# An attention backward kernel: transposing each key block's E in its own step, and X's transposes behind them

## The chip, the cores and the metric

The kernel runs on one core of one Trainium2 chip, as one launch. The metric is the device time of that launch in microseconds (us); less is better. The kernel before took 2694.29 us as the median of three runs (2686.12 to 2701.21).

## What is computed

The reference is a small block, forward and backward: a layer norm, 32-head attention `s`, a gated MLP `g`, and `x + s * g`, together with the gradients for `x`, the attention's weights and the MLP's weights. The part that matters here is the attention.

```python
B, S, D, H = 1, 2048, 512, 32          # Dh = 16
qkv = transpose((x @ wqkv).reshape(B, S, 3, H, Dh), 2, 0, 3, 1, 4)
scores = einsum("bhqd,bhkd->bhqk", q, k) * (Dh ** -0.5)
p = softmax(scores, axis=-1)
o = einsum("bhqk,bhkd->bhqd", p, v)
...
out, vjp = jax.vjp(f, A_x, A_wqkv, A_wo, B_w1, B_b1, B_w2, B_b2)
grads = vjp(grad_out)
```

The backward of attention needs, for every head, the products of two S x S matrices: the unnormalized softmax E, and G, which is E times the matrix of gradients d. Sums over keys (the output, the gradient of q) use them with keys on the partitions; sums over queries (the gradients of k and v) need them with queries on the partitions. So both matrices are made once and transposed once.

## The kernel before

The kernel has three stages: the projections and the MLP forward; the attention, forward and backward in one; the remaining gradients. Only the attention, `attention_core`, is touched. There the order of the instructions of each engine is the order in which the program issues them, written out by hand; the framework adds the waits for data and for buffers.

**Tiling.** Two heads make a pair; there are 16 pairs. 2048 queries are cut into 4 chunks `qc` of 512. A pair with a chunk is a block `j`, of which there are 64. In a block the 2048 keys are 16 key blocks `kb` of 128. One step `g` of the main loop deals with one key block (`j = g // 16`, `kb = g % 16`), so there are 1024 steps and a few more at the end to drain. Four key blocks make a key chunk `kc`.

**What one step issues**, for both heads `hj`, in this order:

- `emit_z(g + ZOFF)` (line 804): matmuls of an older block that add to `Z`, the gradients of k and v, from transposed G (`gk`, on even steps) and transposed E (`ek`, on odd steps). In 16 steps it goes through two halves `kp` of the keys with four query blocks `qb` each. `emit_acc` (lines 817 and 819, VectorE) adds a finished `Z` to `acc` every eighth step. After the last query chunk GpSimd copies the sum to `ob` and SyncE stores it.
- `emit_s(g + 1, 0)` (L629, L635): the scores of the next key block into a PSUM tile `s` of the pool `ps_st`, and ScalarE's exponential of it into the tile `et`, which holds E of one key chunk: 4 query blocks x 4 key blocks x 2 heads x 128.
- `emit_XT(g)`, once per block, at `g % 16 == FIN_AT`: four f32 transposes of `xs`, the sums over keys of the block that has just ended (L744), into a PSUM tile of the pool `ps_d`.
- `emit_d(g, 0)` and `emit_d(g, 1)` (L647): the matmul d of this key block, in tiles of `ps_d`; then `emit_s(g + 1, 1)`.
- `emit_mult(g)` (L660): VectorE writes G = d times E into `gts`, a tile for two key blocks.
- `emit_fin(g)`, once per block, at `FIN_AT`: VectorE copies XT into `xt` and makes reciprocals and factors (L756 to L770), GpSimd makes the weights `W1` and `W2` for Z and writes the block's output and gradient of q.
- `emit_T(g)` (L694): TensorE transposes of E, 128 x 128 each, into a tile of `ps_st`.
- `emit_x(g - 1, ...)` (L719, L722, L725): the sums over keys, into `X`; `emit_xs` (L734), once per block, copies X to `xs` on ScalarE.
- `emit_cT(g)` (L704): ScalarE copies the transposes from PSUM to `ek`.
- `emit_dmat(g)`: DMA transposes on SyncE's queue. After every second key block it transposes `gts` into `gk` (L674). After every fourth, it transposes one query block of `et` into an `ek` (L678), behind the `gk` of the same step.

**How E gets transposed before.** A key chunk has 4 query blocks x 8 squares (4 key blocks, 2 heads). Query block 3 goes by DMA. Query blocks 0 to 2 go over TensorE once the chunk is complete: `t_unit` shifts by four steps, so that step 4, 5 and 6 after the chunk's first step transpose query blocks 0, 1 and 2, eight squares each, and the fourth step transposes nothing.

**Buffers.** `ps_st` and `ps_d` have three PSUM tiles each, `ps_x` and `ps_z` one each. `et` comes from `etp` with 3 buffers, `gts` from `gtp` with 3, `gk` from `gbp` with 7, `ek` from `ekp` with 19, `xs` and `xt` have one each. `FIN_AT` is 2 and `ZOFF` is -21.

**Operands.** Those of the next pair are loaded during the second query chunk (`kb == 0 and qc == 1`): in five parts, four steps apart, three loads, GpSimd copies into `Pad`, a DMA transpose of it to `KVT`, copies again, and a DMA transpose to `QDT`.

Of the kernel before, what the change touches and what calls it, by code (L numbers as in the profile page):

```python
# [542 lines left out]
def attention_core(ctx, tc, NAT_s, NATQ_s, Oall, dQall, dKVT_out, ident_f32, ident_bf, npairs=16, nqc=4):  # L543
# [4 lines left out]
    ps_d = ctx.enter_context(tc.tile_pool(name="ps_d", bufs=3, space=PSUM))  # L548
    ps_x = ctx.enter_context(tc.tile_pool(name="ps_x", bufs=1, space=PSUM))
    ps_z = ctx.enter_context(tc.tile_pool(name="ps_z", bufs=1, space=PSUM))  # L550
    etp = sb("etp", 3)
    gtp = sb("gtp", 3)
    gbp = sb("gbp", 7)
    ekp = sb("ekp", 19)
    xsp = sb("xsp", 1)
    finp = sb("finp", 1)
    wp = sb("wp", 2)
# [51 lines left out]
    def a_unit(g):  # L609
        return (g // 16, g % 16) if 0 <= g < NSTEP else None  # L610
# [53 lines left out]
    def emit_dmat(g):  # L664
        a = a_unit(g)
        if a is None:
            return
        j, kb = a
        kc = kb // 4
        if kb % 2 == 1:  # L670
            h = (kb // 2) % 2
            if h == 0:
                blk[j]["Gk"][kc] = gbp.tile([128, 2, 16, 128], bf16, name="gk")
            nc.sync.dma_start_transpose(out=blk[j]["Gk"][kc][:, h], in_=st_gt[g][:].rearrange("k a h q -> k (a h q)"))  # L674
        if kb % 4 == 3:
            ek = ekp.tile([128, 8, 128], bf16, name="ek")
            blk[j]["Ek"][(kc, 3)] = ek
            nc.sync.dma_start_transpose(out=ek[:], in_=st_et[g][:, 3].rearrange("k a h q -> k (a h q)"))  # L678

    def t_unit(g):  # L680
        a = a_unit(g - 4)
        if a is None or a[1] % 4 == 3:
            return None
        return a[0], a[1] // 4, a[1] % 4

    def emit_T(g):
        u = t_unit(g)
        if u is None:
            return
        j, kc, qb = u  # L690
        et = st_et[j * 16 + kc * 4 + 3]
        t = ps_st.tile([128, 8, 128], bf16, name="tT", tag="st")
        for b in range(8):
            nc.tensor.transpose(t[:, b, :], et[:, qb, b // 2, b % 2, :], ident_bf[:])  # L694
        st_T[g] = t

    def emit_cT(g):
        u = t_unit(g)
        if u is None:
            return  # L700
        j, kc, qb = u
        ek = ekp.tile([128, 8, 128], bf16, name="ek")
        blk[j]["Ek"][(kc, qb)] = ek
        nc.scalar.copy(out=ek[:].rearrange("q a k -> q (a k)").bitcast(f32),  # L704
                       in_=st_T.pop(g)[:].rearrange("q a k -> q (a k)").bitcast(f32))

    def emit_x(g, part):
        a = a_unit(g)
# [19 lines left out]
    def emit_xs(g):  # L728
        a = a_unit(g)
        if a is None or a[1] != 15:  # L730
            return
        j = a[0]
        xs = xsp.tile([128, 512], f32, name="xs")
        nc.scalar.copy(out=xs[:], in_=blk[j].pop("X")[:])  # L734
        blk[j]["xs"] = xs

# [10 lines left out]
    def emit_fin(g):  # L747
        j = g // 16 - 1
        if g % 16 != FIN_AT or not 0 <= j < NB:
            return  # L750
        p, qc = blocks[j]
        NQq = op_of(j)["NATQq"]
        NQd = op_of(j)["NATQd"]
        XT = blk[j].pop("XT")
        xt = finp.tile([128, 4, 128], f32, name="xt")
        nc.vector.tensor_copy(out=xt[:], in_=XT[:])  # L756
        XTv = xt[:].rearrange("q b (r c) -> q b r c", r=4)
        W1 = wp.tile([128, 4, 2, 32], bf16, name="W1")
        W2 = wp.tile([128, 4, 2, 32], bf16, name="W2")
        nc.gpsimd.memset(W2[:, :, :, 0:16], 0.0)  # L760
        st0 = qc * 4
        nqs = NQq[:, st0:st0 + 4, :, 1:17]
        ndo = NQd[:, st0:st0 + 4, :, :]
        bc = lambda ap: ap.to_broadcast([128, 4, 2, 16])
        rL = finp.tile([128, 4, 2, 1], f32, name="rL")
        nc.vector.reciprocal(out=rL[:], in_=XTv[:, :, 2:4, 17:18])  # L766
        dl = finp.tile([128, 4, 2, 1], f32, name="dl")
        nc.vector.tensor_tensor(out=dl[:], in0=XTv[:, :, 2:4, 0:1], in1=rL[:], op=ALU.mult)
        ndr = finp.tile([128, 4, 2, 1], f32, name="ndr")
        nc.vector.scalar_tensor_tensor(out=ndr[:], in0=dl[:], scalar=-1.0, in1=rL[:], op0=ALU.mult, op1=ALU.mult)  # L770
        nc.gpsimd.tensor_tensor(out=W2[:, :, :, 16:32], in0=nqs, in1=bc(rL[:]), op=ALU.mult)  # L771
        nc.gpsimd.tensor_tensor(out=W1[:, :, :, 0:16], in0=ndo, in1=bc(rL[:]), op=ALU.mult)
        nc.gpsimd.tensor_tensor(out=W1[:, :, :, 16:32], in0=nqs, in1=bc(ndr[:]), op=ALU.mult)
        Ov = Oall[:, st0:st0 + 4, p * 32:(p + 1) * 32].rearrange("q b (h c) -> q b h c", h=2)
        nc.gpsimd.tensor_tensor(out=Ov, in0=XTv[:, :, 0:2, 16:32], in1=bc(rL[:]), op=ALU.mult)
        t1 = finp.tile([128, 4, 2, 16], f32, name="t1")
        nc.gpsimd.tensor_tensor(out=t1[:], in0=XTv[:, :, 0:2, 0:16], in1=bc(dl[:]), op=ALU.mult)
        nc.gpsimd.tensor_tensor(out=t1[:], in0=XTv[:, :, 2:4, 1:17], in1=t1[:], op=ALU.subtract)
        rL4 = finp.tile([128, 4, 2, 1], f32, name="rL4")
        nc.gpsimd.tensor_scalar(out=rL4[:], in0=rL[:], scalar1=0.25, scalar2=None, op0=ALU.mult)  # L780
        dQv = dQall[:, st0:st0 + 4, p * 32:(p + 1) * 32].rearrange("q b (h c) -> q b h c", h=2)
        nc.gpsimd.tensor_tensor(out=dQv, in0=t1[:], in1=bc(rL4[:]), op=ALU.mult)
        blk[j]["W1"] = W1
        blk[j]["W2"] = W2

    def emit_z(g):
        u = z_unit(g)
        if u is None:
            return
        j, kp, qb, part = u  # L790
        if part == 0 and qb == 0:
            blk[j]["Z"] = ps_z.tile([128, 512], f32, name="Z", tag="z")
        Z = blk[j]["Z"]
        for par in range(2):
            kc = 2 * kp + par
            if part == 0:
                W = blk[j]["W2"]
                mv = blk[j]["Gk"][kc][:].rearrange("q a (r h b) k -> q h b a r k", r=2, h=2)[:, :, qb]
            else:
                W = blk[j]["W1"]  # L800
                mv = blk[j]["Ek"].pop((kc, qb))[:].rearrange("q (a h) k -> q h a k", h=2)
            for hj in range(2):
                r = 64 * par + 32 * hj
                nc.tensor.matmul(Z[r:r + 32, :], lhsT=W[:, qb, hj, :], rhs=mv[:, hj],  # L804
                                 start=(part == 0 and qb == 0), stop=(part == 1 and qb == 3), skip_group_check=True,
                                 tile_position=(0, r))

    def emit_acc(g):
        u = z_unit(g)
        if u is None or u[2] != 3 or u[3] != 1:  # L810
            return
        j, kp = u[0], u[1]
        p, qc = blocks[j]
        Z = blk[j]["Z"]
        av = acc[:, kp, :]
        if qc == 0:
            nc.vector.tensor_copy(out=av, in_=Z[:])
        else:
            nc.vector.tensor_tensor(out=av, in0=Z[:], in1=av, op=ALU.add)  # L819
        if qc == nqc - 1:  # L820
            if kp == 0:
                cur["ob"] = outp.tile([128, 2, 512], bf16, name="ob")
            ob = cur["ob"]
            nc.gpsimd.tensor_copy(out=ob[:, kp, :], in_=av)
            if kp == 1:
                def store():
                    dv = dKVT_out[p * 64:(p + 1) * 64, :].rearrange("r (a b s) -> r a b s", a=2, b=2)
                    for b in range(2):
                        nc.sync.dma_start(out=dv[:, :, b, :], in_=ob[b * 64:(b + 1) * 64])
                late.append((cur["g"] + 2, store))  # L830

    FIN_AT = 2
    ZOFF = -21
    late = []
    for f in load_ops(0):
        f()
# [2 lines left out]
    for g in range(NSTEP + 16 + 8):  # L839
        cur["g"] = g  # L840
        a = a_unit(g)
        if a is not None:
            j, kb = a
            p, qc = blocks[j]
            if kb == 0 and qc == 1 and p + 1 < npairs:
                for i, f in enumerate(load_ops(p + 1)):
                    late.append((g + 1 + 4 * i, f))
        for it in [x for x in late if x[0] <= g]:
            late.remove(it)
            it[1]()  # L850
        emit_z(g + ZOFF)
        emit_acc(g + ZOFF)
        emit_s(g + 1, 0)
        emit_XT(g)
        emit_d(g, 0)
        emit_d(g, 1)
        emit_s(g + 1, 1)
        emit_mult(g)
        emit_fin(g)
        emit_T(g)  # L860
        emit_x(g - 1, "l")
        emit_x(g - 1, "e")
        emit_x(g - 1, "g")
        emit_xs(g - 1)
        emit_cT(g)
        emit_dmat(g)
        st_gt.pop(g - 2, None)
        st_et.pop(g - 12, None)
# [104 lines left out]
```

## Time and profile before

| | |
|---|---|
| median of three runs | 2694.29 us |
| the profiled execution | 2689.98 us |
| its span | 2688.2 us |
| mean granted TensorE clock | 0.957 |
| TensorE matmul, busy | 2294.1 us (85%) |
| VectorE, busy | 1898.4 us (71%) |
| ScalarE, busy | 1795.7 us (67%) |
| GpSimd, busy | 600.7 us (22%) |
| first and last d of the attention | 283.5 and 2072.9 us |

The profile shows one execution on the core. PE is TensorE's matmuls, PEld its loads of weights, DVE is VectorE, ACT ScalarE, POOL GpSimd, SP SyncE; SPq rows are DMAs that SyncE issues. "L694" is line 694 of the kernel. Rows of the groups read: line, engine, operation, what is written <- what is read, shapes, count | busy us, mean ns of one | idle time of the engine just ahead of them, and what ended it. Rows of the timeline read: start, duration, engine, line, operation, tiles, count and, in brackets, idle time with its releaser. A few of the attention's groups in the whole span:

```profile
L635 ACT ACTIVATE et<-s 128x512 bf16<-128x512 f32 x2048 | 1127.3, 596 | 247.9 <-PE s L629 136.7
L694 PE MATMUL tT<-ident_bf,et 128*128 128x128 bf16 x6144 | 475.2, 220 | 40.1 <-ACT ek L704 39.4
L704 ACT COPY ek<-tT 128x512 f32<-128x512 f32 x768 | 455.2, 593 | 0.5 <-PE tT L694 0.5
L725 PE MATMUL X<-gts,NAT 128*17 128x512 bf16 x2048 | 393.4, 380 | 0.0
```

Matmuls are pipelined, and their durations are modelled, so that the time of a set of them is read from the start of one to the start of the next set. ScalarE and VectorE overlap the end of one instruction with the start of the next, and there too the distance from start to start is what a row of them costs.

### The profile page before, as it was taken

The numbers are of one execution on the slowest core, as the hardware profiler recorded it, in microseconds if no ns is written. First come the engines' busy times: TensorE is split into PE (matmuls) and PEld (weight loads), VectorE is DVE, ScalarE is ACT, GpSimd is POOL, SyncE is SP. The second block draws the span as 40 slices with busy tenths as digits, with TensorE's granted clock in tenths as the row PEclk, the third lists the DMA queues.
The fourth block names the chain that finished last, engine by engine and source line by source line (L and its number), as shares of the span: only waits on it lengthen the run. The fifth ranks groups of instructions, "written<-read, shape, count | busy, mean of one in ns | idle before, by whom it ended". The sixth has DMA issues, their size and how long they took to land. (4 is left out here: it accounts for less than half of the span.)

```text
span 2688.2 us, 61100 instructions
## 1 busy us (share of the span) xinstructions
PE 2294.1 (85%) x24005; PEld 1054.0 (39%) x24064; DVE 1898.4 (71%) x3190; ACT 1795.7 (67%) x3317; POOL 600.7 (22%) x990
## 2 busy tenths in 40 slices
PE   3788799999999999999999999999999656656967
PEld 2333244444444444444444444444444333322433
DVE  5766687878788778787787877778787368860144
ACT  3344688888888888888888888888887254430110
POOL 0434111011110111101111011110111258850034
PEclk8899899999999999999999999999999878878989
DMA  5343999999999999999999999999999633327331
GB/s 188 94 128 126 186 199 212 195 211 204 204 216 193 211 204 204 215 196 215 201 202 215 191 214 202 205 209 198 210 198 182 229 109 103 103 72 185 116 111 43
DMA packets 1564740, 477.08 MB, mean 177 GB/s; under 512 B 1484706, under 2 KB 1549603, under 8 KB 1564451
## 3 DMA queue, kind: packets, MB, share of 16 engines
q1 hardware_dynamic: 1491058, 419.56, 78.5%
q10 hardware_dynamic: 73392, 53.62, 6.5%
q8 instruction: 188, 3.08, 0.5%
q14 instruction: 102, 0.83, 0.1%
HBM read 65.41 MB, written 55.32 MB: 45 GB/s over the span
## 5 line engine op out<-in xcount | busy, mean ns | idle before, releaser
L660 DVE TENSOR_TENSOR gts<-d,et 128x512 bf16<-128x512 f32 x2048 | 1292.3, 683 | 364.1 <-PE s L629 200.1
L635 ACT ACTIVATE et<-s 128x512 bf16<-128x512 f32 x2048 | 1127.3, 596 | 247.9 <-PE s L629 136.7
L629 PE MATMUL s<-QDT,KVT 32*128 32x512 bf16 x2048 | 528.0, 386 | 17.7 <-DMA QDT<-Pad 16.1
L647 PE MATMUL d<-QDT,KVT 32*128 32x512 bf16 x2048 | 489.9, 383 | 54.0 <-DVE gts L660 53.7
L694 PE MATMUL tT<-ident_bf,et 128*128 128x128 bf16 x6144 | 475.2, 220 | 40.1 <-ACT ek L704 39.4
L704 ACT COPY ek<-tT 128x512 f32<-128x512 f32 x768 | 455.2, 593 | 0.5 <-PE tT L694 0.5
L694 PEld LDWEIGHTS <-et 128*128 128x128 bf16 x6144 | 354.2, 98 | 213.1 <-issue 199.2
L722 PE MATMUL X<-et,NAT 128*32 128x512 bf16 x2048 | 404.0, 392 | 0.0
L719 PE MATMUL X<-et,Lc 128*32 128x512 bf16 x2048 | 403.4, 391 | 0.0
L725 PE MATMUL X<-gts,NAT 128*17 128x512 bf16 x2048 | 393.4, 380 | 0.0
L629 PEld LDWEIGHTS <-KVT 32*128 32x128 bf16 x2048 | 145.3, 91 | 555.1 <-issue 523.8
L804 PE MATMUL Z<-ek,W 128*32 128x512 bf16 x2048 | 300.8, 380 | 0.0
L804 PE MATMUL Z<-gk,W 128*32 128x512 bf16 x2048 | 289.6, 380 | 1.3 <-DVE acc L819 1.3
L771 POOL TENSOR_TENSOR W<-NATQq,rL 128x128 bf16<-128x128 bf16 x64 | 25.7, 401 | 1178.3 <-DVE rL L766 1178.3
L804 PEld LDWEIGHTS <-W 128*32 128x32 bf16 x4096 | 199.7, 96 | 125.9 <-issue 31.2
L719 PEld LDWEIGHTS <-Lc 128*32 128x32 bf16 x2048 | 98.2, 93 | 139.0 <-issue 59.6
L647 PEld LDWEIGHTS <-KVT 32*128 32x128 bf16 x2048 | 96.0, 91 | 11.4 <-issue 11.4
L722 PEld LDWEIGHTS <-NAT 128*32 128x32 bf16 x2048 | 98.6, 93 | 0.0
L421 PE MATMUL dh_tp<-ident_bf,dh 128*128 128x128 bf16 x224 | 31.0, 278 | 77.9 <-DVE dh L418 75.5
L725 PEld LDWEIGHTS <-NAT 128*17 128x17 bf16 x2048 | 95.3, 90 | 0.0
L448 PE MATMUL ps_dw<-dm_all,hgc 128*128 128x512 bf16 x220 | 54.0, 402 | 29.6 <-DMA hgc<-HG_s 29.4
L427 PE MATMUL ps_dy<-w1T,dh1T 128*128 128x512 bf16 x208 | 67.8, 471 | 3.7 <-ACT dh1T L422 3.4
(197 smaller groups left out, 2442.2 us busy)
## 6 DMA issues: line engine op xcount, KB each, us to landing
gk<-gts SPq DMA_TRANSPOSE x512, 4.2
HG_s<-hg SPq DMA_DIRECT2D x16, 448.0 KB, 2.9
DH_s<-dh ACTq DMA_DIRECT2D x16, 448.0 KB, 2.5
NAT<-NAT_s SPq DMA_DIRECT2D x16, 264.0 KB, 3.3
GB_s<-gB ACTq DMA_DIRECT2D x16, 256.0 KB, 2.0
ek<-et SPq DMA_TRANSPOSE x256, 3.1
dKVT_s<-ob SPq DMA_DIRECT2D x32, 128.0 KB, 2.5
dhc<-DH_s ACTq DMA_DIRECT2D x2, 2048.0 KB, 13.7
```

The costliest lines, as they stand in the source:

```text
L427: nc.tensor.matmul(ps[:], lhsT=dh1T[:, fc, :], rhs=w1T[:, fc, :], start=(fc == 0), stop=(fc == FC - 1))
L448: nc.tensor.matmul(ps[:], lhsT=hgc[:, t, :], rhs=dm_all[:, t, :], start=(t == 0), stop=(t == NT - 1))
L629: nc.tensor.matmul(s[:], lhsT=op["KVT"][r:r + 32, kb * 128:(kb + 1) * 128], rhs=op["QDT"][r:r + 32, qc * 512:(qc + 1) * 512], start=True, ...
L635: nc.scalar.activation(out=et[:, :, kb % 4, hj, :], in_=s[:].rearrange("k (b q) -> k b q", b=4), func=ACT.Exp)
L647: nc.tensor.matmul(d[:], lhsT=op["KVT"][r:r + 32, kb * 128:(kb + 1) * 128], rhs=op["QDT"][r:r + 32, qc * 512:(qc + 1) * 512], start=True, ...
L660: nc.vector.tensor_tensor(out=gts[:, kb % 2, hj, :].rearrange("k (b q) -> k b q", b=4), in0=st_d.pop((g, hj))[:].rearrange("k (b q) -> k b ...
L694: nc.tensor.transpose(t[:, b, :], et[:, qb, b // 2, b % 2, :], ident_bf[:])
L704: nc.scalar.copy(out=ek[:].rearrange("q a k -> q (a k)").bitcast(f32), in_=st_T.pop(g)[:].rearrange("q a k -> q (a k)").bitcast(f32))
L719: nc.tensor.matmul(X[64 + 32 * hj:96 + 32 * hj, :], lhsT=Lc[:], rhs=et[:, :, kb % 4, hj, :], start=(kb == 0), stop=False, skip_group_check ...
L722: nc.tensor.matmul(X[32 * hj:32 * hj + 32, :], lhsT=NATt[:, kb, hj, 1:33], rhs=et[:, :, kb % 4, hj, :], start=(kb == 0), stop=(kb == 15), ...
L725: nc.tensor.matmul(X[64 + 32 * hj:64 + 32 * hj + 17, :], lhsT=NATt[:, kb, hj, 0:17], rhs=st_gt[g][:, kb % 2, hj, :], start=False, stop=(kb ...
L804: nc.tensor.matmul(Z[r:r + 32, :], lhsT=W[:, qb, hj, :], rhs=mv[:, hj], start=(part == 0 and qb == 0), stop=(part == 1 and qb == 3), skip_ ...
```

## The change

The transposes of E move from the completed key chunk to the single key block. In every step, TensorE transposes six squares of that step's own key block (query blocks 1 to 3, two heads) into a PSUM tile of 128 x 3 x 2 x 128; ScalarE copies it, 128 x 384 as f32, into a new tile `ek` of a whole key chunk, from the pool `ekc` with 7 buffers. The DMA transposes query block 0 in place of 3, from the same place in SyncE's queue, into `ek0` from `ekp[0]` with 5 buffers.

`emit_T` is issued behind the second `emit_s`, and `emit_XT` behind `emit_T`; before, XT stood between the first `s` and `d`. `FIN_AT` becomes 1 and `ZOFF` -20, so that the block's finish comes one step earlier, and Z one step earlier.

`etp` goes from 3 buffers to 2. `xt` is taken from the buffer of `xs`. `ob` becomes a tile for one half `kp`, with a store of its own for each half, so that there are 64 stores of half the size in place of 32.

```diff
-    etp = sb("etp", 3)
+    etp = sb("etp", 2)
-    ekp = sb("ekp", 19)
+    ekp = [sb("ekp0", 5)]
+    ekc = sb("ekc", 7)
...
         if kb % 4 == 3:
-            ek = ekp.tile([128, 8, 128], bf16, name="ek")
-            blk[j]["Ek"][(kc, 3)] = ek
-            nc.sync.dma_start_transpose(out=ek[:], in_=st_et[g][:, 3].rearrange("k a h q -> k (a h q)"))
-
-    def t_unit(g):
-        a = a_unit(g - 4)
-        if a is None or a[1] % 4 == 3:
-            return None
-        return a[0], a[1] // 4, a[1] % 4
+            ek = ekp[0].tile([128, 4, 2, 128], bf16, name="ek0")
+            blk[j]["Ek"][(kc, 0)] = ek
+            nc.sync.dma_start_transpose(out=ek[:].rearrange("q a h k -> q (a h) k"), in_=st_et[g][:, 0].rearrange("k a h q -> k (a h q)"))

     def emit_T(g):
-        u = t_unit(g)
-        if u is None:
-            return
-        j, kc, qb = u
-        et = st_et[j * 16 + kc * 4 + 3]
-        t = ps_st.tile([128, 8, 128], bf16, name="tT", tag="st")
-        for b in range(8):
-            nc.tensor.transpose(t[:, b, :], et[:, qb, b // 2, b % 2, :], ident_bf[:])
+        a = a_unit(g)
+        if a is None:
+            return
+        kk = a[1] % 4
+        et = st_et[g]
+        t = ps_st.tile([128, 3, 2, 128], bf16, name="tT", tag="st")
+        for qb in range(1, 4):
+            for hj in range(2):
+                nc.tensor.transpose(t[:, qb - 1, hj, :], et[:, qb, kk, hj, :], ident_bf[:])
         st_T[g] = t

     def emit_cT(g):
...
+        if kk == 0:
+            cur["ek"] = ekc.tile([128, 3, 4, 2, 128], bf16, name="ek")
+            blk[j]["Ek"][kc] = cur["ek"]
+        nc.scalar.copy(out=cur["ek"][:, :, kk].rearrange("q b h k -> q b (h k)").bitcast(f32),
+                       in_=t[:].rearrange("q b h k -> q b (h k)").bitcast(f32))
...
-        xs = xsp.tile([128, 512], f32, name="xs")
+        xs = xsp.tile([128, 512], f32, name="xs", tag="xs")
...
-        xt = finp.tile([128, 4, 128], f32, name="xt")
+        xt = xsp.tile([128, 4, 128], f32, name="xt", tag="xs")
...
-                mv = blk[j]["Ek"].pop((kc, qb))[:].rearrange("q (a h) k -> q h a k", h=2)
+                mv = blk[j]["Ek"][(kc, 0)][:] if qb == 0 else blk[j]["Ek"][kc][:, qb - 1]
+                mv = mv.rearrange("q a h k -> q h a k")
...
-            if kp == 0:
-                cur["ob"] = outp.tile([128, 2, 512], bf16, name="ob")
-            ob = cur["ob"]
-            nc.gpsimd.tensor_copy(out=ob[:, kp, :], in_=av)
...
+            ob = outp.tile([128, 512], bf16, name="ob")
+            nc.gpsimd.tensor_copy(out=ob[:], in_=av)
...
-    FIN_AT = 2
-    ZOFF = -21
+    FIN_AT = 1
+    ZOFF = -20
...
         emit_s(g + 1, 0)
-        emit_XT(g)
         emit_d(g, 0)
         emit_d(g, 1)
         emit_s(g + 1, 1)
+        emit_T(g)
+        emit_XT(g)
         emit_mult(g)
         emit_fin(g)
-        emit_T(g)
```

More of the change, by code (lines that the diff above doesn't have):

```diff
@@ L675, in emit_dmat @@
         if kb % 4 == 3:
-            ek = ekp.tile([128, 8, 128], bf16, name="ek")
-            blk[j]["Ek"][(kc, 3)] = ek
-            nc.sync.dma_start_transpose(out=ek[:], in_=st_et[g][:, 3].rearrange("k a h q -> k (a h q)"))
-    def t_unit(g):
-        a = a_unit(g - 4)
-        if a is None or a[1] % 4 == 3:
-            return None
-        return a[0], a[1] // 4, a[1] % 4
+            ek = ekp[0].tile([128, 4, 2, 128], bf16, name="ek0")
+            blk[j]["Ek"][(kc, 0)] = ek
+            nc.sync.dma_start_transpose(out=ek[:].rearrange("q a h k -> q (a h) k"), in_=st_et[g][:, 0].rearrange("k a h q -> k (a h q)"))
     def emit_T(g):
-        u = t_unit(g)
-        if u is None:
+        a = a_unit(g)
+        if a is None:
             return
-        j, kc, qb = u
-        et = st_et[j * 16 + kc * 4 + 3]
-        t = ps_st.tile([128, 8, 128], bf16, name="tT", tag="st")
-        for b in range(8):
-            nc.tensor.transpose(t[:, b, :], et[:, qb, b // 2, b % 2, :], ident_bf[:])
+        kk = a[1] % 4
[4 more added lines that the diff above has]
+                nc.tensor.transpose(t[:, qb - 1, hj, :], et[:, qb, kk, hj, :], ident_bf[:])
         st_T[g] = t
     def emit_cT(g):
-        u = t_unit(g)
-        if u is None:
+        a = a_unit(g)
+        if a is None:
             return
[L701 to L705, printed above, removed]
+        j, kb = a
+        kc, kk = kb // 4, kb % 4
+        t = st_T.pop(g)
+        if kk == 0:
[3 more added lines that the diff above has]
+                       in_=t[:].rearrange("q b h k -> q b (h k)").bitcast(f32))
     def emit_x(g, part):
@@ L820, in emit_acc, with store @@
         if qc == nqc - 1:
-            if kp == 0:
-                cur["ob"] = outp.tile([128, 2, 512], bf16, name="ob")
-            ob = cur["ob"]
-            nc.gpsimd.tensor_copy(out=ob[:, kp, :], in_=av)
[L825 to L830, printed above, removed]
-    FIN_AT = 2
-    ZOFF = -21
+            ob = outp.tile([128, 512], bf16, name="ob")
+            nc.gpsimd.tensor_copy(out=ob[:], in_=av)
+            def store():
+                dv = dKVT_out[p * 64:(p + 1) * 64, :].rearrange("r (a b s) -> r a b s", a=2, b=2)
+                for b in range(2):
+                    nc.sync.dma_start(out=dv[:, kp, b, :], in_=ob[b * 64:(b + 1) * 64, :])
+            late.append((cur["g"] + 2, store))
+    FIN_AT = 1
+    ZOFF = -20
     late = []
```

## The prediction

> **What bounds the kernel now.** I read the page first (parts 1, 2 and 3), then the stretches by engine, the groups of the attention stage, the waits, and last the timeline of one block. Part 2 shows three stages; the attention stage is the long middle one.
>
> ```profile
> span 2688.2 us, 61100 instructions
> PE 2294.1 (85%) x24005; PEld 1054.0 (39%) x24064; DVE 1898.4 (71%) x3190; ACT 1795.7 (67%) x3317; POOL 600.7 (22%) x990
> PE   3788799999999999999999999999999656656967
> DMA  5343999999999999999999999999999633327331
> ```
>
> TensorE and the DMA rows read 9 in 26 and 27 of 40 slices. The first d of attention starts at 283.5 us and the last at 2072.9, so 64 blocks of 16 steps take about 28.02 us each, 1793 us in all; only this part is changed. One quiet block, in the view by stretches (span, then busy time per engine):
>
> ```profile
> 1177.98:1205.57 27.59, 26.39 (x326) 11.78 (x326) 22.40 (x39) 23.86 (x46) 3.66 (x10) 1.00 1.01 190
> ```
>
> 27.59 us is the usual block; the mean is 0.43 higher because operand loads fall into one block of four. No engine is full, but PE is nearest. Its steps, from the starts of d in the timeline: 1.635 us with eight transposes, 1.081 without (1179.80, the start of such a set, to the next):
>
> ```profile
> 1179.80 0.39 PE L629 MATMUL s<-QDT,KVT 32*128 32x512 bf16 x1
> 1180.84 0.61 PE L694 MATMUL tT<-ident_bf,et 128*128 128x128 bf16 x8 [0.65 <-ACT ek L704]
> ...
> 1182.45 0.66 PE L744 MATMUL XT<-ident_f,xs 128*128 128x128 f32 x4
> 1183.04 0.39 PE L647 MATMUL d<-QDT,KVT 32*128 32x512 bf16 x2
> ...
> 1186.87 0.37 PE L647 MATMUL d<-QDT,KVT 32*128 32x512 bf16 x1 [0.54 <-DVE gts L660]
> ```
>
> Unhindered, 12 x 1.635 + 4 x 1.081 = 23.94 us. The other 3.65 us: step 1 takes 3.24 (+1.60: transposes wait 0.65 for ACT's copy behind xs, and XT stands between s and d, 0.9 us), step 4 takes 2.56 (+0.93: d waits for DVE, which does the block's finish and acc there), and 1.1 lies in small waits of d for DVE around the short step. DVE needs 0.598 us from one multiply to the next, 1.196 a step, more than the short step has.
>
> **The change part by part.**
> *Transposes.* (1.635 - 1.081)/8 = 69 ns each. Before 12 x 8, after 16 x 6: 96 a block both ways. A step becomes 1.081 + 6 x 0.069 = 1.497, a block 23.95. The work is the same; only waits can change. DVE's 1.196 then fits every step.
>
> *The ACT copy.* The page's rows for 128x512 (592 ns, L704) and for 128x256 (372 ns, a CAST from f32 of the same engine) give 0.86 ns an element, so 128x384 takes 482, and from its start to the next instruction 478 - 110 = 368. ACT per step: 494 + 477 + 368 = 1.34 us, not full.
>
> The Trainium skill (Perfetto Trace Analysis, "Optimizing Scalar/DVE Operations") says grouping into larger operations helps throughput if the engine is saturated, with about 51 ns of overhead per ScalarE access of PSUM, which speaks against 1024 copies in place of 768: by it 256 x 0.051 = 13 us more ACT work, an estimate from that page. ACT's 23.86 of 27.59 us is not saturated, so by the row this costs the end nothing.
>
> *The chain through three PSUM buffers.* ps_st has 3 buffers and every step now takes 3 (two s, one T), so T of a step waits for the copy of the step before. That chain: s to exponential 0.44 (1186.87 to 1187.31), second exponential 0.494, copy 0.477 later, 0.482 long, 0.05 to T: 1.943 us from s to the next T. PE goes from T to the next s in 1.497 - 0.32 = 1.178 (0.32: s and d before T). If T follows its s by x, the next does so by 1.943 - 1.178 - x = 0.765 - x, at least 0.32; mean 0.38. A step is 1.178 + 0.38 = 1.56 and 16 are 24.96. Before, the short step breaks this chain every fourth step.
>
> *xs, XT, the finish, acc.* xs (0.48) still stands before a copy, in step 0: T of step 1 comes 0.54 late. XT now stands behind T, where it no longer parts s from d: between 0.59 (1182.45 to 1183.04) and 0.91 as before; I take 0.59, as T and XT both fill the array. Together 1.13, less 0.06 that the chain above gains: 1.07. The finish adds 1.41 us to DVE (597+784+238+200+190 between starts, less the 0.6 of the multiply itself), in step 1, behind XT, which stretches that step: DVE has caught up before step 3's d. acc at step 3 comes on top: d waits 0.18, of which 0.06 is absorbed; acc at step 11 is hidden by DVE's spare 0.36 a step. Were DVE late, d and then s would follow, as at 1186.87. W1 and W2 are ready at about 3.9 us after d of step 1; Z asks in step 4, about 5 us after. So without DMA 24.96 + 1.07 + 0.12 = 26.15.
>
> *Buffers.* xt in xs's buffer, the ob tile by halves, ekp, ekc: Z reads the oldest ek a step or two before it is overwritten; nothing waits. The stores become 64 of half the size: 32 more SP issues of 592 ns, all in blocks that follow a pair, put ahead of the transpose of step 13 or 5, into SP's idle time (2.8 us at 1184.55 to 1187.44). Bound: 19 us if none were hidden; I take 0.
>
> *etp from 3 to 2: the part that decides.* The exponential of unit 4c+8 overwrites the tile that unit 4c+3 closed. That tile's last reader is the DMA transpose ek on SP's queue, behind the gk of the same step, which waits for the multiply.
>
> ```profile
> L674 SPq DMA_TRANSPOSE gk<-gts x512: 1316/1773/3778, 288.6 to 2074.7; - x171
> DMA to landing us min/median/max: 3.7/4.2/7.0
> L678 SPq DMA_TRANSPOSE ek<-et x256: 1232/1317/2943, 293.8 to 2076.5; - x128
> DMA to landing us min/median/max: 2.8/3.1/5.6
> q8 instruction: 188, 3.08, 0.5%
> ```
>
> (Issue, then landing: least, median, most.) A multiply pair ends 0.52 + 1.29 = 1.81 after its d, an exponential starts 0.44 after its s, and s and d go together: from the multiply of 4c+3 to the exponential of 4c+8 are 4 steps less 1.37, or 4.87 us at 1.56 a step. The trace of before has 4.84 to 4.94 there in three chunks of four, 6.38 in the one with XT; but with three buffers nothing depended on it. What must fit: 0.03 + issue of gk 1.77 + 0.09 + landing of ek 3.1 = 5.0 by medians, 4.2 by the least, 9.4 by the most. Followed chunk by chunk (158 of blocks without loads): 10% under 4.8, median 5.7, 90% under 6.9; the 95 with nothing ahead in the queue: 4.7, 5.4, 6.7, half near 4.8 and near half above 6. Chunks in which a packet of the instruction queue ran have median 6.1, those without 4.8.
>
> So some 45% of chunks overrun by about 1.4 us. A late exponential doesn't delay the multiply in front of it, so with two buffers the next wait is shorter by as much: 0.45/1.45 of chunks wait, 0.44 on average, 0.5 with the small ones; 0.2 in the chunk that holds XT. 3 x 0.5 + 0.2 = 1.7 a block. Bounds: 0 if ek always lands as at the least; 2.4 from the landing times of all chunks, without the absorbing. What waits behind that exponential: on ACT the copy, so T; then s, X, Z.
>
> The Trainium skill (DMA: Bandwidth & Descriptors, "Latency and other measured facts") gives 261 GB/s for DMA_TRANSPOSE; the row of this block has 190, so by that rule the queue has room (an estimate), no exponential waits, and the sum ends at 26.15. I go by the landing times: it is one transfer's delay, not the rate, that must fit into 4.87 us.
>
> *Loads.* In the four chunks with operand transposes on SP, ek lands 6.7, 9.0, 7.0 and 6.6 us after the multiply (medians). Against 4.87, with the same alternation, 1.9 + 2.3 + 0 + 1.3 = 5.5, less the 1.7 counted: 3.8 per four blocks, 0.95 a block; before they cost 0.43. I take 0.75, since part of that lateness is the old kernel's own jam.
>
> *Sum.* 26.15 + 1.7 + 0.75 = 28.6 against 28.02: +0.58 x 64 = +37 us. The profiled execution took 2689.98 (span 2688.2), the median of the runs is 4.3 above it; on the median 2694.29 + 37 = about 2730.
>
> **The rivals.**
> *A, faster: ek lands in time.* If the even steps keep the queue clear and landing stays at 4.6 to 4.9, the waits go: 26.15 + 0.43 = 26.6, -1.4 x 64 = 2694 - 91 = 2603; with a third of the waits left 27.2, 2640. For it: half of undisturbed chunks. Against it: instruction packets come as before, the other half.
> *B, clearly slower: every chunk waits.* Landing times of all chunks plus loads in full, 26.15 + 2.4 + 0.95 = 29.5, 2789; more if gk falls behind and multiplies wait too (that wait, 20.7 us in 12 cases between 700 and 1800, exists now). It decides from a mean landing above 6 us; the mean of the undisturbed chunks is 5.6.
> *C, a draw:* smoothing and waits cancel, 28.0: 2694. It needs 1.1 of waits.
>
> **How the numbers follow.** Forecast (slower, 2705 to 2770) 0.42; A 0.34; B 0.13; C 0.11. Half a percent (13 us) is what a measurement of this kernel tells from no change. Faster 0.34, same 0.11, slower 0.42 + 0.13 = 0.55. Signs are mixed, so the range is wide: 2598 takes in A up to its best, 2800 most of B.
>
> **What would show it.** Right: idle time of ACT before an exponential put down to DMA ek; no 0.54 waits of d; steps of 1.56; a 128x384 copy near 482 ns; T to T of step 1 about 1.1 us longer. Wrong: no exponential behind a DMA (A), copies over 550 ns, d still waiting for DVE, or transposes spread so that a step is over 1.65 without any DMA wait.

## The result and the profile after

The changed kernel took 2802.84 us as the median of four runs (2784.51 to 2804.47), against 2692.22 us for the kernel before beside it. The ratio is 1.0393, with a 95% interval of 1.034 to 1.0445: 3.9% slower, some 110 us by the medians. The forecast was slower, by 37 us, and 2730 us.

The page of the changed kernel (span, busy time by engine, TensorE and DMA in 40 slices):

```profile
span 2801.5 us, 61402 instructions
PE 2356.9 (84%) x24064; PEld 1065.6 (38%) x24064; DVE 1923.1 (69%) x3190; ACT 1778.8 (63%) x3573; POOL 601.3 (21%) x990
PE   3687799999989999889999999999999857765967
DMA  5434899999999999999999999999999753226331
```

TensorE does the work of before, and the attention is longer: its first d starts at 286.8 us, its last at 2188.9, so 1902 us in place of 1789. The mean granted clock of the profiled execution is 0.933, 0.957 before. Nothing else moved: ahead of it 287 us (283 before), behind it 613 (615). A block takes 29.79 us on average, 27.98 before. Two groups of the kernel before, and then those of the changed kernel, say where the time went:

```profile
L629 PE MATMUL s<-QDT,KVT 32*128 32x512 bf16 x2048 | 528.0, 386 | 17.7 <-DMA QDT<-Pad 16.1
L647 PE MATMUL d<-QDT,KVT 32*128 32x512 bf16 x2048 | 489.9, 383 | 54.0 <-DVE gts L660 53.7
```

```profile
L636 ACT ACTIVATE et<-s 128x512 bf16<-128x512 f32 x2048 | 1117.0, 600 | 377.8 <-DMA ek<-et 174.7
L630 PE MATMUL s<-QDT,KVT 32*128 32x512 bf16 x2048 | 484.5, 392 | 136.1 <-ACT et L636 109.9
L690 PE MATMUL tT<-ident_bf,et 128*128 128x128 bf16 x6144 | 527.4, 223 | 36.1 <-ACT ek L703 35.9
L703 ACT COPY ek<-tT 128x384 f32<-128x384 f32 x1024 | 501.6, 490 | 0.8 <-PE tT L690 0.6
L648 PE MATMUL d<-QDT,KVT 32*128 32x512 bf16 x2048 | 423.3, 394 | 3.6 <-DVE gts L661 3.6
```

The exponential had 247.9 us of idle time before, ended mostly by s, and never by ek. Now it has 377.8, and ek ended 174.7 of them. The next row hands this on: s waited 17.7 us before, nearly all of it for one DMA, and 136.1 now, 109.9 of them for that exponential. The last row is a part of what the change gained: d, which waited 54.0 us, 53.7 of them for the multiplies, waits 3.6. The copy takes 490 ns; 482 was worked out.

One such wait, in the timeline of the changed kernel, SP first and then ACT and PE:

```profile
1228.76 1.33 SPq L679 DMA_TRANSPOSE ek<-et  x1
```

```profile
1231.42 0.48 ACT L703 COPY ek<-tT 128x384 f32<-128x384 f32 x1
1233.77 1.08 ACT L636 ACTIVATE et<-s 128x512 bf16<-128x512 f32 x2 [1.87 <-DMA ek<-et]
1234.75 0.48 ACT L703 COPY ek<-tT 128x384 f32<-128x384 f32 x1
```

```profile
1232.61 0.59 PE L804 MATMUL Z<-gk,W 128*32 128x512 bf16 x4
1234.42 0.37 PE L630 MATMUL s<-QDT,KVT 32*128 32x512 bf16 x1 [1.22 <-ACT et L636]
```

The transpose was issued at 1228.76 and released the exponential at 1233.77. TensorE had work until 1233.20 and then stood for 1.22 us, with everything else behind s.

From the starts of d, by medians, the steps that nothing disturbs alternate between 1.523 and 1.588 us, a mean of 1.556 (1.56 was worked out), step 1 takes 2.617 (worked out: 1.56 + 1.07), step 4 takes 1.774 (1.56 + 0.12). The steps that hold these waits are 3 to 4, 7 to 8, 11 to 12 and 15 to 0, where the exponential of units 4, 8, 12 and 0 (the unit is the key block `kb`) takes a tile that ek must have left. All 118 waits for ek are there.

### The profile page after: what moved, and what is told of

It is laid out like the page before. It is cut to its first block, busy times and chain, and to the rows that moved or that the text cites. A ratio compares the mean times of both kernels' runs of the same rounds, so it can differ in the third digit from the quotient of the medians.

```text
span 2801.5 us, 61402 instructions
## 1 busy us (share of the span) xinstructions
PE 2356.9 (84%) x24064; PEld 1065.6 (38%) x24064; DVE 1923.1 (69%) x3190; ACT 1778.8 (63%) x3573; POOL 601.3 (21%) x990
## 5 line engine op out<-in xcount | busy, mean ns | idle before, releaser
L661 DVE TENSOR_TENSOR gts<-d,et 128x512 bf16<-128x512 f32 x2048 | 1311.0, 683 | 435.7 <-PE s L630 200.7
L636 ACT ACTIVATE et<-s 128x512 bf16<-128x512 f32 x2048 | 1117.0, 600 | 377.8 <-DMA ek<-et 174.7
L630 PE MATMUL s<-QDT,KVT 32*128 32x512 bf16 x2048 | 484.5, 392 | 136.1 <-ACT et L636 109.9
L690 PE MATMUL tT<-ident_bf,et 128*128 128x128 bf16 x6144 | 527.4, 223 | 36.1 <-ACT ek L703 35.9
L690 PEld LDWEIGHTS <-et 128*128 128x128 bf16 x6144 | 384.1, 99 | 342.8 <-issue 326.7
L703 ACT COPY ek<-tT 128x384 f32<-128x384 f32 x1024 | 501.6, 490 | 0.8 <-PE tT L690 0.6
L648 PE MATMUL d<-QDT,KVT 32*128 32x512 bf16 x2048 | 423.3, 394 | 3.6 <-DVE gts L661 3.6
L804 PE MATMUL Z<-ek,W 128*32 128x512 bf16 x2048 | 311.5, 391 | 0.0
L630 PEld LDWEIGHTS <-KVT 32*128 32x128 bf16 x2048 | 119.3, 91 | 469.8 <-issue 469.8
L804 PEld LDWEIGHTS <-W 128*32 128x32 bf16 x4096 | 209.1, 98 | 126.0 <-issue 31.1
L648 PEld LDWEIGHTS <-KVT 32*128 32x128 bf16 x2048 | 96.2, 91 | 107.6 <-issue 107.0
```

Source lines behind the costliest of these rows:

```text
L630: nc.tensor.matmul(s[:], lhsT=op["KVT"][r:r + 32, kb * 128:(kb + 1) * 128], rhs=op["QDT"][r:r + 32, qc * 512:(qc + 1) * 512], start=True, ...
L636: nc.scalar.activation(out=et[:, :, kb % 4, hj, :], in_=s[:].rearrange("k (b q) -> k b q", b=4), func=ACT.Exp)
L648: nc.tensor.matmul(d[:], lhsT=op["KVT"][r:r + 32, kb * 128:(kb + 1) * 128], rhs=op["QDT"][r:r + 32, qc * 512:(qc + 1) * 512], start=True, ...
L661: nc.vector.tensor_tensor(out=gts[:, kb % 2, hj, :].rearrange("k (b q) -> k b q", b=4), in0=st_d.pop((g, hj))[:].rearrange("k (b q) -> k b ...
L690: nc.tensor.transpose(t[:, qb - 1, hj, :], et[:, qb, kk, hj, :], ident_bf[:])
L703: nc.scalar.copy(out=cur["ek"][:, :, kk].rearrange("q b h k -> q b (h k)").bitcast(f32), in_=t[:].rearrange("q b h k -> q b (h k)").bitcas ...
```

## The experiments

Each ran beside the kernel before on one chip; differences in us between two of them are of medians. Ratios are to that kernel, with 95% intervals.

**Who waits for ek: its place, and the tiles.** Three runs.

`e1_ek_first`, the changed kernel:

```diff
     def emit_dmat(g):
...
+        if kb % 4 == 3:
+            ek = ...
+            nc.sync.dma_start_transpose(out=ek..., in_=st_et[g][:, 0]...)
         if kb % 2 == 1:
...
             nc.sync.dma_start_transpose(out=blk[j]["Gk"][kc][:, h], in_=st_gt[g]...)
-        if kb % 4 == 3:
-            ek = ...
-            nc.sync.dma_start_transpose(out=ek..., in_=st_et[g][:, 0]...)
```

> The changed kernel with one thing moved: in the last step of a key chunk the DMA transpose of E (ek) is issued ahead of that of G (gk). Theory: the time is lost because the exponential waits for ek to have read its E tile (two buffers), and ek stands in SyncE's queue behind a gk that waits for the multiply. In front of it, ek starts some 1.8 + 1.8 us earlier, lands well inside the 4.9 us, and the 175 us of ACT's idle time put down to DMA ek go to under 20. A block is then 26.2 us plus 0.5 for operand loads: 900 + 64 x 26.7 = about 2610 (2590 to 2640). Rival, the chain through the three PSUM tiles or the new order itself is what costs: 2770 to 2800. Rival, the DMA queue as a whole is too full, so that gk lands late in ek's place and the multiplies wait for gts: 2700 to 2800, with idle time of DVE put down to DMA gk.

Measured: 2632.54 us, ratio 0.9787 (0.9769 to 0.9806). Idle time of the exponential for ek fell from 174.7 to 30.3 us. Who waited for which DMA (us in all, times, longest), in the changed kernel and then in that with ek first:

```profile
ACT et L636 <- DMA ek<-et: 174.7, 118, 3.5
...
DVE gts L661 <- DMA gk<-gts: 6.2, 4, 2.2
```

```profile
DVE gts L661 <- DMA gk<-gts: 61.0, 50, 3.4
...
ACT et L636 <- DMA ek<-et: 30.3, 26, 2.8
```

So the same instructions in another order on one queue are worth 170 us. It stays 22 us above what the theory gave: a quiet block is 26.2 us, as the median of two of the four query chunks, but the mean of all blocks is 27.10, and a part of the waits has moved to gk, which was rarely late in the changed kernel (6.2 us).

`e2_et_three`, the changed kernel with the third tile:

```diff
-    etp = sb("etp", 2)
+    etp = sb("etp", 3)
...
-        k.dQall = pO.tile([128, NT, D], bf16, name="dQall")
+        k.dQall = k.Oall
```

> The changed kernel with three E tiles (etp 3, as before the change). To make room, the attention's output and the gradient of q share one tile, so one overwrites the other; the instructions are the same. Theory (the wait for ek with two tiles): no idle time of ACT for DMA ek, about 2610, as with ek issued first. Rival (the order or the PSUM chain): 2770 to 2800. If this one is faster than with ek first, the place of ek costs gk something; if slower, something else in the queue counts.

Measured: 2648.63 us, ratio 0.9839 (0.982 to 0.9859). The output and the gradient of q share one tile here, so this kernel leaves one of them out, and it stands for its time alone. No exponential waits for ek any more. DVE's waits for gk are 69.6 us:

```profile
DVE gts L661 <- DMA gk<-gts: 69.6, 43, 3.9
```

Two tiles cost the change 154 us (2802.84 - 2648.63).

`e3_before_et_two`, the kernel before with one line of the change:

```diff
-    etp = sb("etp", 3)
+    etp = sb("etp", 2)
```

> The kernel before with one thing taken from the change: two E tiles in place of three. Theory: the same wait appears, since ek lands 5.8 us (median) after the multiply and the exponential comes 4.9 after it in three chunks of four: some 1.7 to 2.5 us a block, 2690 + 110 to 160 = 2800 to 2850. Rival (two tiles are enough, the new step is what is slow): 2690.

Measured: 2831.0 us, ratio 1.0517 (1.0485 to 1.0549). The same wait appears, 108.5 us in 66 cases:

```profile
ACT et L635 <- DMA ek<-et: 108.5, 66, 2.9
```

One buffer less makes the old kernel slower than the whole change does. The three runs agree: the loss comes with the wait for ek, and rivals that blame the new step fall.

**The order of the steps alone.** `e5_before_XT_behind`, the kernel before:

```diff
         emit_s(g + 1, 0)
-        emit_XT(g)
         emit_d(g, 0)
         emit_d(g, 1)
         emit_s(g + 1, 1)
+        emit_T(g)
+        emit_XT(g)
         emit_mult(g)
         emit_fin(g)
-        emit_T(g)
```

> The kernel before with the issue order of the change alone: transposes of E behind the second s, X's transposes behind them. Theory: XT no longer parts s from d: 0.3 us a block, 2690 - 20 = 2670. Rival: nothing gained (2690), since DVE's finish in step 2 to 4 ends last, or a loss of up to 20 us because XT takes its PSUM tile later and the finish comes later.

Measured: 2650.54 us, ratio 0.9846 (0.9827 to 0.9866): 41 us, twice what was expected. Step 1 goes from 3.24 to 2.34 us and step 4 from 2.56 to 2.34, step 2 from 1.64 to 2.08. As the transposes of E keep their place among TensorE's own instructions, what this moves is X's transposes (XT). The whole change with three tiles takes as much, 2649, but its parts differ: its undisturbed blocks take 26.18 us, 26.72 here, so that six transposes in every step do shorten them. The blocks with operand loads lose that again, 29.96 on average against 28.67, and the multiplies' waits for gk are 69.6 us against 53.8.

**ek first without need.** `e6_before_ek_first`, the kernel before with the two DMA transposes exchanged as in the first run.

> The kernel before with ek issued ahead of gk and nothing else. Theory: with three E tiles nothing waits for ek, so the order alone gives nothing: 2680 to 2700. Rival: ek first is a gain of its own (as much as the 170 us between the changed kernel and that with ek first), by letting gk run more evenly: under 2660.

Measured: 2688.54 us, ratio 0.9992 (0.9982 to 1.0003). Where three tiles leave room, the order is worth nothing.

**Why the wait is so long: the multiply ahead of it.** In the changed kernel a multiply pair ends 1.81 us after its d in most steps, but 2.385 in step 3, where acc follows the block's finish, and 2.003 in step 11, behind the other acc. gk and ek of these units start that much later. The mean waits of the exponentials of units 0, 4, 8 and 12 are 0.79, 0.13, 1.13 and 0.68 us. `e4_z_later`:

```diff
-    ZOFF = -20
+    ZOFF = -21
```

> The changed kernel with Z and acc one step later (ZOFF -21, as before the change). Theory on the size: the wait of the exponential of unit 8 (1.14 us on average, against 0.7 for units 0 and 12) is long because acc falls on the multiply of unit 3, which ends 2.39 us after its d in place of 1.81, and gk and then ek start that much later; acc at step 11 does the same by 0.2 to unit 11. With acc a step later these multiplies end at 1.8 to 1.9, the waits of units 8 and 0 fall to 0.7 and 0.6, less what the later wait of the next chunk takes back: 0.3 to 0.6 us a block, 2802 - 20 to 40 = 2765 to 2785. Rival: acc's place counts for nothing (2795 to 2805), or Z, now nearer to the end of its buffers, costs more (above 2805).

Measured: 2750.2 us, ratio 1.0223 (1.0203 to 1.0242), some 50 us below the change. The multiplies of units 3 and 11 now end 1.812 us after their d, and the waits are 0.61, 0.10, 0.90 and 0.47. The idle time for ek is 133.5 us, 41 less. So the place of Z and acc counts, by more than was expected (20 to 40). Unit 8 stays the longest, and unit 12 fell too, whose multiply acc did not delay.

**What the wait costs beyond its length.** The block's loss against an undisturbed one is 29.79 - 26.17 = 3.6 us, but ACT's waits for ek are only 174.7/64 = 2.7. This sum does not part the wait from all else: against the whole blocks of the kernels with ek first (27.10) and with three tiles (27.44) the loss is 2.7 and 2.3, but there the multiplies wait for gk. What happens behind a wait is seen in two stretches of the changed kernel, by engines, with granted clock, DMA share and GB/s in the last three columns (two steps ahead of a wait of 1.75 us, and two steps behind it):

```profile
1250.19:1253.30 3.11, 3.11 (x42) 1.37 (x41) 2.58 (x5) 2.73 (x7) 0.00 (x0) 1.00 1.46 215
1258.03:1261.20 3.17, 3.17 (x27) 1.06 (x25) 1.29 (x2) 1.59 (x4) 0.00 (x0) 0.52 0.50 107
```

TensorE is busy throughout both. In about the same 3.1 us it does 42 matmuls at a clock of 1.00 and 27 at 0.52, while the DMA share is down from 1.46 to 0.50. In its timeline, ahead and behind:

```profile
1253.64 0.49 PE L690 MATMUL tT<-ident_bf,et 128*128 128x128 bf16 x6
...
1255.99 0.37 PE L630 MATMUL s<-QDT,KVT 32*128 32x512 bf16 x1 [1.09 <-ACT et L636]
...
1258.50 0.82 PE L690 MATMUL tT<-ident_bf,et 128*128 128x128 bf16 x6
```

The clock's records of the attention have 135 us at 0.5: 32 stretches of 3.41 or 6.83 us, and 9 us of one that began ahead of the first d. The kernel before has 11.6 us: one stretch of 3.41 and the rest of one from ahead of the first d. Half of 135 - 11.6 is 62 us, or 0.97 a block. That is the most that a half clock can cost. Seven undisturbed steps (9 or 13 of their block) that lie whole in such a stretch take 2.69 us in place of 1.52; by that the 126 us in those 32 stretches lose an estimated 55, or 0.86 a block. `e11_T_twice` puts work into the gaps:

```diff
+        for rep in range(2 if kk == 3 else 1):
             for qb in range(1, 4):
                 for hj in range(2):
                     nc.tensor.transpose(t[:, qb - 1, hj, :], et[:, qb, kk, hj, :], ident_bf[:])
```

> The changed kernel with the six transposes of the last step of each key chunk done twice, into the same PSUM tile with the same result: 256 x 0.416 = 106 us more TensorE work, put just ahead of the place where TensorE stands when the exponential waits for ek. Theory (the wait is dearer than its own length, because the granted clock halves for 3.4 us behind many gaps of TensorE over 1.0 us): half of the chunks wait, and there the extra work costs nothing and shortens a gap of some 1.25 us to 0.85; the other half pays, 256 x 0.54 x 0.42 = 58 us; time at half clock falls from 135 us to some 40, which gives back 47. 2803 + 10 = 2813 (2795 to 2830), with the exponential's idle time for ek falling from 175 to about 120. Rival, the clock behind the gaps costs little: 2803 + 58 = 2861 (2845 to 2875).

Measured: 2778.99 us, ratio 1.0314 (1.0272 to 1.0356). With 106 us more work the kernel is not slower than the changed one; its median is 24 us lower, but the two intervals overlap. Time at half clock is 39 us, and the idle time for ek is 125.3; both are what was expected.

```profile
ACT et L636 <- DMA ek<-et: 125.3, 93, 3.7
```

The time lies far below the rival's 2845 to 2875, in which the clock costs little, and below the theory's range too. It came out 34 us below the forecast for it: step 4, where d waited for acc, falls from 1.774 to 1.523 us, since the added work stands ahead of that wait too (16 us), and the rest isn't accounted for. From the windows view, 700 to 1800 us, the changed kernel, then the one with the transposes twice:

```profile
700.00:1800.00 1100.00, 1006.64 (x11982) 440.26 (x11974) 841.87 (x1406) 872.63 (x1813) 146.56 (x390) 0.97 1.01 194
```

```profile
700.00:1800.00 1100.00, 1034.32 (x13064) 487.85 (x13062) 858.25 (x1427) 887.57 (x1839) 147.75 (x396) 0.99 1.02 196
```

ACT, whose work per step is the same in both, gets 1839 instructions done in place of 1813.

**Toward a better version.** Three runs from the kernel with ek first.

`e7_ek_first_split_loads`: each operand transpose in two halves (`[plain, ck, tk(0), tk(1), cq, tq(0), tq(1)]`).

> The kernel with ek issued first, and the two operand transposes of 512 KB cut into halves, four steps apart. What still stands there is 61 us of DVE and 30 us of ACT idle for DMA gk and ek, most of it in the block with the loads and the one after it (28.5 and 27.4 us against 26.2). If one long transpose ahead of gk makes it, halves take half of that away: 2632 - 20 to 40 = 2592 to 2612. Rival: the halves issue and land no faster together, the queue is as late: 2625 to 2640.

Measured: 2626.46 us, ratio 0.9766 (0.9747 to 0.9786). This overlaps the interval of ek first alone, so a gain isn't shown. The block with the loads falls from 28.48 to 27.43 us, the next rises from 27.43 to 27.88: the waits are spread, not removed.

`e8_X_ahead_of_T`:

```diff
+        emit_x(g - 1, "l")
+        emit_x(g - 1, "e")
         emit_T(g)
         emit_XT(g)
         emit_mult(g)
         emit_fin(g)
-        emit_x(g - 1, "l")
-        emit_x(g - 1, "e")
         emit_x(g - 1, "g")
```

> The kernel with ek issued first, and the first four X matmuls of a step ahead of the transposes instead of behind them. Theory: steps alternate between 1.523 and 1.588 us because T waits for the copy of the step before (one PSUM tile); 0.22 us of X ahead of T is more than the 0.13 that the wait can be, so that a step is PE's own 1.497: 0.94 us a block, 2632 - 60 = 2570. Rival: the steps stay at 1.52 to 1.59 because something else sets them (2625 to 2640), or X ahead of T delays XT and the finish (above 2640).

Measured: 2666.64 us, ratio 0.9911 (0.9892 to 0.993), 34 us worse than ek first. The alternation is gone, as the theory said: most steps take 1.631 us (step 1 takes 2.40, steps 3 and 4 1.79), and no T waits for a copy. But TensorE's own step has become longer: the median step of 1.631 has no idle time of TensorE in it. Its timeline:

```profile
1240.69 0.39 PE L718 MATMUL X<-et,Lc 128*32 128x512 bf16 x2
1240.70 0.39 PE L721 MATMUL X<-et,NAT 128*32 128x512 bf16 x2
1241.02 0.51 PE L690 MATMUL tT<-ident_bf,et 128*128 128x128 bf16 x6
1241.46 0.39 PE L724 MATMUL X<-gts,NAT 128*17 128x512 bf16 x2
1241.47 0.60 PE L804 MATMUL Z<-ek,W 128*32 128x512 bf16 x4
```

The four X take 0.33 us here, from 1240.69 to T at 1241.02; where the next X follows them directly, 0.22 (1250.96 to 1251.18 in the changed kernel). That is most of the difference to the 1.497 worked out for TensorE's own step.

`e10_best`: ek first, split operand transposes and ZOFF -21.

> ek issued first, operand transposes in halves, and Z with acc one step later (ZOFF -21). Theory: with the wait for ek gone, the later acc is worth only the wait of d that it causes in step 4: 1.776 to 1.526 us, 0.25 us a block, 2626 - 16 = 2610 (2600 to 2618). Rival: acc at step 12 and 4 meets other waits and gives nothing (2622 to 2632); or it is worth as much as in the kernel with ek behind gk, 52 us (2575).

Measured: 2629.83 us, ratio 0.9782 (0.975 to 0.9813). Step 4 is 1.524 us, as expected, and the time is the same: steps 7, 9 and 13 have become longer on average (1.71, 1.73 and 1.73 against 1.55, 1.58 and 1.60 in `e7_ek_first_split_loads`), and the multiplies' waits for gk are 75.7 us against 54.2. The best versions therefore lie at 2626 to 2633 us, 2.1 to 2.3% below the kernel before.

## Why the prediction was right and where it was wrong

**Right: the mechanism and its sign.** Transposes of equal cost, a step of 1.56 us by the chain through three PSUM tiles, XT behind T, d no longer waiting for DVE: 26.15 us was worked out for a block without DMA waits, and the median steps of the kernel with ek first add up to 26.17. The exponential that waits for ek with two E tiles is shown by three runs. That a wait makes the next one shorter is there too: behind a wait of over 0.5 us another such follows in 17% of the chunks (16 of 96), behind none in 50% (68 of 137).

**Wrong: the term "etp from 3 to 2", 1.7 us a block and 0.75 for loads.** These 2.45 us were all that the sum had for waits on DMAs. Measured against the undisturbed block, it is 3.6, 74 us more over the attention. Two things were missing in the term.

*The price of a wait was taken as its length.* The length was nearly right: ACT's idle time for ek is 2.0 us in the first and last of a pair's four blocks, where 1.7 was worked out, and the loads add 0.73 on average (0.75 was worked out), 2.73 in all. The other 0.9 us of the 3.6 are lost beyond that idle time. Behind its longer gaps TensorE ran at half clock, by the estimates above 55 to 62 us, or 0.86 to 0.97 a block, which is about what is missing. The kernel before had one such stretch of its own in the attention, and the prediction didn't price them. That the gaps set the half clock off is shown by the doubled transposes, under which 135 us of it became 39; how much of the 0.9 us it makes is an estimate, and a part may be time that transfers cost the kernel with three tiles as well.

*The multiply was taken to end 1.81 us after its d in every chunk.* The prediction saw that the finish and acc push the multiply of step 3, and charged d for it, 0.18; it didn't carry that into the start of gk and ek. In the first and last blocks unit 8, which waits for the ek behind that multiply, waits 1.0 us, where 0.5 was worked out. With Z and acc a step later the idle time for ek falls by 41 us.

A smaller slip: the mean block of the kernel before was read as 28.02 us and is 27.98, which would have raised the forecast by 3 us; the longest path to ek's landing adds up to 9.5 us, not 9.4, and nothing rests on it.

The landing times themselves were sized well: from the multiply to ek's landing the prediction had 5.6 us on average for undisturbed chunks, and it is 5.6 in the changed kernel in blocks without loads. Chunks in which a packet of the larger instruction queue ran have a median of 6.2 there, those without one 5.0; that these packets are the cause was not tried.

**The rivals.** A (ek lands in time) is what happens once ek is issued first: 2632 against the 2603 to 2640 worked out. B (2789) came nearest to the measured time, but not as told: not every chunk waits, 46% do, and the block loses more than the waits' length. C, the draw, didn't come.

**The skill's rules.** The Trainium skill (DMA: Bandwidth & Descriptors, "Latency and other measured facts") gives 261 GB/s for a DMA transpose with a non-contiguous middle dimension. This rate, by which no exponential would wait, didn't tell what happens: the changed kernel's transfers moved 194 GB/s between 700 and 1800 us, and TensorE still stood until one of them had landed. With ek first they move 212.

The Trainium skill (Perfetto Trace Analysis, "Optimization Strategy") says that the same gap, repeated on the engine that should be saturated, can mean too little buffer space for the next tile. The 118 waits at the same four units, which TensorE's s then waits for, and which are gone with one tile more, agree.

## What to carry to other kernels

When a buffer is taken away, find the last reader of each tile and work out when that reader starts, not only how long it takes: here the reader stood in a queue behind a DMA that waited for another engine. Putting the transfer that frees a buffer ahead of one that doesn't was worth 170 us and cost no memory. Price a new wait on TensorE by its length and by what its clock does behind it: here an estimated 0.9 to 1.0 us a block on top of 2.7.

## What the runs showed of the hardware

The granted clock halves behind short gaps. In the changed kernel's attention, of 64 gaps of TensorE of 1.0 to 2.6 us, 33 had a stretch at 0.5 that began in them or within 3.5 us behind them; of 94 gaps of 0.3 to 1.0 us, 2 did. The stretches last 3.41 or 6.83 us. All 32 begin on one grid of 3.413 us, and in this trace they go by TensorE's idle time within a window of that grid: of the windows at full clock, none of the 457 with under 1.02 us of it in all was followed by one at half clock, of 36 with 1.02 to 1.37 us 8 were, and of 26 with more 24. The kernel before with two E tiles shows the same (0 of 494, 5 of 35, 13 of 14). So a gap that two windows share can pass. The Trainium skill (TensorE: Matmul & The Clock Gate, "HAM oscillation — how this bites in real kernels") gives the rule as no idle gap over about 3.4 us. The lengths of the stretches agree with its window, the threshold doesn't: gaps of 1.0 to 1.5 us were enough in 19 of 46 cases.

Four X matmuls, which use 32 columns of the array each (128*32 in the rows), took 0.33 us where six transposes of 128*128 followed them, and 0.22 where more X did. With the same instructions the step became 1.631 us, in place of 1.523 to 1.588. That the change of shape is the cause was not tried by itself.
